# Attention and a gated feed-forward block: a new order of the steps, and GpSimd waiting for VectorE at a port that both use

## The chip, the cores and the metric

The kernel runs on one core of one Trainium2 chip. The metric is the device time of one execution in microseconds (us); it is given as the median of three runs. The engines are TensorE (PE; its weight loads are PEld), VectorE (DVE), ScalarE (ACT), GpSimd (POOL) and SyncE (SP), which issues all DMAs here.

## The reference

Attention over 8 batches of 12 heads, 448 positions and 64 columns, with `q` and `k` normalised by row, then a feed-forward block with a convolution of three taps over the sequence inside its gate:

```python
def rmsnorm(x, g):
    rms = np.sqrt(np.mean(x * x, axis=-1, keepdims=True) + 1e-06)
    return x / rms * g
q_n, k_n = (rmsnorm(q, g_q), rmsnorm(k, g_k))
scores = scale * np.matmul(q_n, k_n.transpose(0, 1, 3, 2))
attn = softmax(scores)
x = np.matmul(attn, v)          # 8 x 448 x 768 after heads are joined
h = np.maximum(x @ w_in, 0.0)   # 768 -> 1024
gate = 1.0 / (1.0 + np.exp(-conv3(h)))
out = h * gate @ w_out          # 1024 -> 768
```

## The kernel before

Two heads form a pair; there are 48 pairs `n`, six of them a batch `b`. A pair is loaded as rows of `q`, `k` and `v`. Its `q` and `k` are squared (`square`), summed (`square_sum`, L396) and turned into a factor by nine small steps (`rsqrt`, L404; L417 to L432 are its instructions), with which `apply_rms` (L440) multiplies them; that product is recorded under the helper's line L110 with the tile `sq`. Transposes on TensorE (L456) and copies (`qk_hi`, `qk_lo`, tiles `kT` and `qT`) follow, from pair 10 on a transposing DMA for `q` in place of one of them. `scores` (L642) go to PSUM, seven blocks of rows `j` a pair; for each of them `soft_max` (L648, VectorE) takes the row maximum and `soft_exp` (L656, ScalarE) the exponential with its row sum. From pair 10 on a value is carried as two float16 halves, a high and a low one: `p_hi` copies to float16 and `p_lo` (L669) subtracts the copy from the value, tile `ph`, again under L110; `p_turn` (L676) then transposes both halves by a DMA to tile `PT`. Blocks that are not transposed so go over TensorE (L686). `v_hi` and `v_lo` (L746, instruction at L748, tile `vp`) do the same with `v`; `pv` (L764) multiplies. `sum_add`, `sum_step` and two small DMAs spread the reciprocal row sums (`rB`), `x_scale` (L775) applies them, `x_hi` and `x_lo` (L786) split the result.

The feed-forward block of a batch starts when its six pairs are done: `in_part` (L848) and `out_part` (L917) are its matmuls, three for each product of halves, and `in_relu`, `in_conv`, `in_tanh`, `in_gate`, `in_hi`, `in_lo` work on each of its eight column blocks. Its matmuls are interleaved with the attention of later batches. Its weights arrive as float64 words and are converted by bit operations on VectorE (`convert`, L269, three instructions a part at L221, L225, L229), then bounded: ScalarE takes the largest magnitude of each part (L279), `bound_max` (L286) the largest of all, `bound_turn` (L289) turns it over TensorE (L190), and a power of two scales the weight, which `split` and `rest` cut in halves. `x @ w_in` can start after that.

All of this is some thousands of steps with a time each, a place in a plan (`at`), shifted by the table `SHIFT`. A planner inside the kernel (the loop at L1473) orders them before anything is emitted: it plays the engines forward with a duration for each step from the table `options`, picks on each engine the waiting step with the least sum of start and urgency, and where a step may run on several engines takes the one that would start first, with a patience from `PH` added for the second choice. `shared` (L1460) tells which steps it takes to need the SBUF port that VectorE and GpSimd have in common; before, one such step on either engine held back the other until it was nearly done, in the plan:

```python
            end = t + c
            free[e] = end - OVER[e]
            if shared(e, step[0]):
                port = free[e] - 0.08
```

In the emitted program an engine runs its instructions in the order so found, and waits for another engine only where the data demand it. The plan's port rule thus set the order, and no instruction waited for it.

Of the kernel before, what the change touches and what calls it, by code (L numbers as in the profile page):

```python
# [20 lines left out]
    sw=0.0, f_pl=0.052, f_ql=0.872, f_lo=0.172, f_rms=0.091, f_sq=0.309, T=17.368, ti=41.151,  # L21
    si=4.096, so=8.649, hop=0.891, beta=0.015, wi0=-53.559, wi1=121.264, wo0=27.379,
    wo1=191.814, cw=130.244, p_evac=0.84, p_hi=0.797, p_lo=1.64, p_rms=0.176, p_v=3.888,
    p_x=0.778, p_g=2.422, p_relu=5.177, p_cv=2.905, p_ev=1.195, sp=0.047, nbulk=4, p_rs=0.042,
    p_sq=15.42, p_w=72.367, v0=26.835, nd=6, cs=5, ct=3, cm=9, ne=5, n2=0, n1=10, q1=10, nf=10,
    pvs=4, p_sa=1.065, p_c0=0.206, p_ca=0.624, p_ss=3.937, p_qh=3.454, p_ql=2.719, p_ph=4.9,
    p_pl=4.316,
)
PACE = [
    19.684, 19.21, 17.229, 18.732, 12.899, 14.504, 12.3, 10.264, 22.811, 17.751, 23.834, 17.246,  # L30
]
SHIFT = dict(
    prepare=49.118, load_g=66.183, make_g=161.271, load_cw=41.777, make_cw=228.436, load=30.589,
    convert=88.08, bound=185.211, bound_max=505.945, bound_turn=109.494, bound_row=36.478,
    bound_spread=103.145, scale=368.594, in_factor=602.484, split=143.452, rest=-5.433,
    out_factor=26.564, load_k=207.53, load_q=-22.481, square=411.214, square_sum=340.919,
    rsqrt=50.152, apply_rms=498.265, qk_transpose=555.031, qk_hi=86.942, v_load=355.244,
    v_bound=-7.228, scores=24.319, soft_max=-4.096, soft_exp=21.811, p_transpose=365.136,
    p_evac=1.005, sum_add=366.28, sum_step=2.99, sum_transpose=104.607, sum_evac=262.686,
    sum_store=184.116, sum_load=7.026, pv=384.832, x_scale=90.761, x_hi=276.516, x_lo=5.432,  # L40
    v_max=-27.973, v_turn=484.625, v_row=103.578, v_spread=219.686, v_scale=143.146,
    qk_lo=-5.353, q_hi=-16.467, q_lo=93.092, q_turn=368.336, p_hi=513.085, p_lo=-4.651,
    p_turn=292.059, p_low=-2.554, v_hi=204.989, v_lo=184.473, moe_scales=122.854,
    in_part=120.167, in_relu=338.096, in_conv=209.998, in_tanh=27.902, in_gate=21.022,
    in_hi=197.514, in_lo=1.938, in_carry=175.792, out_scales=185.546, out_part=267.736,
    out_evac=257.905, out_store=1.003,
)
SCHED = {}
# [21 lines left out]
def tile_attention_moe(ctx: ExitStack, tc, q, k, v, g_q, g_k, w_in, conv_w, w_out, out):  # L70
# [1203 lines left out]
    def options(name, *a):  # L1274
# [21 lines left out]
            square=lambda: [act(1.06), pool(1.89)] if a[1] == 2 else [act(0.55), pool(1.05)],  # L1296
            square_sum=lambda: [dve(1.21 if a[1] == 2 else 0.62)],
            rsqrt=lambda: [dve(0.19)] if a[1] == 1 or n0 and not a[2] else [dve(0.19), pool(0.54 if a[1] in (4, 7, 8) else 0.28)],
            apply_rms=lambda: [dve(0.69), pool(1.07)] if n0 else [pool(1.07), dve(0.69)],
            qk_transpose=lambda: [pe(0.42)],  # L1300
            qk_hi=lambda: [act(0.6), dve(0.62)],
            qk_lo=lambda: [dve(0.65)],
# [287 lines left out]
```

## Time and profile before

| | |
|---|---|
| runs, us | 843.82, 840.89, 843.28 (median 843.28) |
| profiled execution, span, us | 844.4 |
| its own time beside the span | not given by the page; the span is the first to the last instruction |
| mean granted clock of TensorE | 0.994 |
| PE / DVE / ACT / POOL busy, us | 799.5 / 701.8 / 698.1 / 517.7 |

The page gives busy time by engine as a union of its instructions' spans. Matmuls overlap each other in the records, so a TensorE that is busy throughout is not at its peak. A row of the timeline gives start, length, engine, line and output<-input; in brackets the idle time before it and what ended that. The chain is followed back from the last instruction.

### The profile page before, as it was taken

The numbers are of one execution on the slowest core, as the hardware profiler recorded it, in microseconds if no ns is written. First come the engines' busy times: TensorE is split into PE (matmuls) and PEld (weight loads), VectorE is DVE, ScalarE is ACT, GpSimd is POOL, SyncE is SP. The second block draws the span as 40 slices with busy tenths as digits, with TensorE's granted clock in tenths as the row PEclk, the third lists the DMA queues.
The fourth block names the chain that finished last, engine by engine and source line by source line (L and its number), as shares of the span: only waits on it lengthen the run. The fifth ranks groups of instructions, "written<-read, shape, count | busy, mean of one in ns | idle before, by whom it ended". The sixth has DMA issues, their size and how long they took to land.

```text
span 844.4 us, 17078 instructions
## 1 busy us (share of the span) xinstructions
PE 799.5 (95%) x5650; PEld 435.0 (52%) x5650; DVE 701.8 (83%) x1298; ACT 698.1 (83%) x1647; POOL 517.7 (61%) x633
## 2 busy tenths in 40 slices
PE   3897999999999999999999999999999999999998
PEld 2454455545554555555555555555545555555554
DVE  7889988997899889998889988998789989781430
ACT  4889999989899887999898987998898987893441
POOL 4445246487678667597577767697667767572120
PEclk9998999999999999999999999999999999999999
DMA  9684553169997899869997898979996899555001
GB/s 255 180 197 122 172 147 109 45 137 197 180 194 173 163 193 200 167 141 196 197 177 161 182 200 186 179 150 199 183 187 154 185 184 169 108 106 112 10 18 58
DMA packets 325640, 132.47 MB, mean 157 GB/s; under 512 B 265312, under 2 KB 321968, under 8 KB 325552
## 3 DMA queue, kind: packets, MB, share of 16 engines
q1 hardware_dynamic: 325552, 131.39, 75.0%
q8 instruction: 44, 0.72, 0.4%
q14 instruction: 44, 0.36, 0.1%
HBM read 56.65 MB, written 11.18 MB: 80 GB/s over the span
## 4 chain that ended last, share of the span: by engine, by line
PE 38%; ACT 24%; DVE 17%; DMA 9%; issue 7%; POOL 4%; SPq 2%; ACTq 0%; DVEq 0%; POOLq 0%
PE bank L917 15%; PE bank L848 8%; PE bank L764 6%; PE bank L642 5%; DMA rB<-rd 4%; ACT ph L98 3%; PE bank L686 3%; ACT sq L385 2%; DMA PT<-ph 2%; DMA wo<-in_moe_w_in_dram 2%; DVE vp L748 1%; ACT PT L98 1%; POOL ph L110 1%; ACT bank L856 1%; SPq L678 1%
## 5 line engine op out<-in xcount | busy, mean ns | idle before, releaser
L848 PE MATMUL bank<-x,wi 128*128 128x448 f16 x1152 | 233.8, 353 | 0.0
L917 PE MATMUL bank<-wo,gring 128*128 128x384 f16 (+1 forms) x1056 | 203.4, 327 | 1.8 <-DVE c_(0_7_1979 L878 1.7
L848 PEld LDWEIGHTS <-wi 128*128 128x128 f16 x1152 | 110.9, 98 | 99.3 <-issue 7.6
L917 PEld LDWEIGHTS <-gring 128*128 128x128 f16 (+1 forms) x1056 | 101.6, 99 | 67.6 <-issue 16.3
L642 PE MATMUL bank<-kT,qT 64*128 64x448 f16 (+3 forms) x1072 | 131.8, 395 | 4.1 <-ACT qT L98 3.4
L764 PE MATMUL bank<-PT,vp 112*64 112x448 f16 x912 | 93.7, 354 | 0.8 <-DVE c_(5_4_8472 L878 0.4
L110 POOL TENSOR_TENSOR x<-x,x 128x448 f16<-128x448 f32 x48 | 52.9, 1102 | 45.3 <-ACT x L98 33.3
L110 POOL TENSOR_TENSOR sq<-qkf,st 112x512 f32<-112x512 f32 x61 | 72.1, 1191 | 8.5 <-DVE st L417 5.1
L764 PEld LDWEIGHTS <-vp 112*64 112x64 f16 x912 | 50.2, 110 | 41.3 <-issue 12.6
L396 DVE TENSOR_REDUCE st<-sq 112x16 f32<-112x1024 f32 (+1 forms) x50 | 58.2, 1168 | 7.0 <-ACT sq L385 6.5
L642 PEld LDWEIGHTS <-qT 64*128 64x128 f16 (+1 forms) x912 | 32.7, 97 | 51.8 <-issue 32.1
L385 ACT ACTIVATE sq<-qkf 112x1024 f32<-112x1024 f32 (+1 forms) x50 | 51.1, 1022 | 4.2 <-DMA qkf<-in_q_dram 2.3
L917 PE MATMUL bank<-wo,wi 128*128 128x384 f16 (+1 forms) x192 | 46.9, 326 | 0.0
L456 PE MATMUL bank<-ident,sq 112*128 112x112 f32 x232 | 32.4, 267 | 14.4 <-POOL sq L110 13.9
L775 DVE TENSOR_TENSOR x<-bank,rB 128x448 f32<-128x448 f32 x38 | 23.6, 622 | 25.2 <-PE bank L764 9.9
L702 DVE TENSOR_TENSOR PT<-bank,PT 112x512 f16<-112x512 f32 x57 | 39.0, 684 | 4.3 <-ACT PT L98 3.9
L856 ACT ACTIVATE bank<-bank 128x448 f32<-128x448 f32 x64 | 34.1, 534 | 7.3 <-PE bank L848 6.6
L748 DVE SCALAR_TENSOR_TENSOR vp<-v,vsc,vp 112x512 f16<-112x512 f32 x38 | 39.8, 1047 | 0.2 <-ACT vp L102 0.2
L98 ACT COPY PT<-bank 112x512 f32<-112x512 f32 x64 | 36.9, 590 | 3.5 <-PE bank L686 3.4
L110 DVE TENSOR_TENSOR sq<-qkf,st 112x512 f32<-112x512 f32 x35 | 38.7, 1131 | 0.0
L709 POOL TENSOR_SCALAR rsum<-rsum 128x7 f32<-128x7 f32 x48 | 17.5, 365 | 33.5 <-ACT e_(3_6_774 L656 7.5
L98 ACT CAST x<-x 128x448 f16<-128x448 f32 x45 | 25.2, 560 | 15.5 <-DVE x L775 14.8
(2228 smaller groups left out, 2021.8 us busy)
## 6 DMA issues: line engine op xcount, KB each, us to landing
qkf<-in_k_dram SPq DMA_DIRECT2D x48, 224.0 KB
v<-in_v_dram SPq DMA_DIRECT2D x48, 224.0 KB
rB<-rd SPq DMA_DIRECT2D x96, 112.0 KB
wo<-in_moe_w_in_dram SPq DMA_DIRECT2D x12, 512.0 KB
gring<-in_moe_w_out_dram SPq DMA_DIRECT2D x16, 384.0 KB
qkf<-in_q_dram SPq DMA_DIRECT2D x24, 224.0 KB
qkf<-in_q_dram SPq DMA_DIRECT2D x48, 112.0 KB
PT<-ph SPq DMA_TRANSPOSE x209
```

What stands on the lines that cost most here:

```text
L98: (nc.scalar.copy if e == "ACT" else elementwise(e).tensor_copy)(dst, src)
L110: elementwise(e).tensor_tensor(dst, a, b, op=op)
L385: nc.scalar.activation(sq, x, AF.Square)
L396: nc.vector.tensor_reduce(st, sq, axis=AX.X, op=ALU.add)
L456: nc.tensor.transpose(ps[:, t * PB : (t + 1) * PB], x[:, t], ident[:PB, :PB])
L642: nc.tensor.matmul(ps[u][o, :S], lhs, rhs, start=(i == 0), stop=(whole(m) or i == 2),)
L702: nc.vector.tensor_tensor(turned(n, j, 1), held["t", ("p", n, j)][:PB].rearrange("p (k q) -> p k q", k=NB), turned(n, j, 0), op=ALU.subtract,)
L748: nc.vector.scalar_tensor_tensor(vp[:, 1], old("v", n), old("vsc", n // NP)[:PB, 1:2], vp[:, 0], op0=ALU.mult, op1=ALU.subtract,)
L764: nc.tensor.matmul(ps[HALF[h], :S], lhs, rhs, start=(i == 0 and k == 0), stop=(i == pvs(n)[-1] and k == NB - 1),)
L848: nc.tensor.matmul(ps[:, :S], wi[:, wl, c, fc * P : (fc + 1) * P], old("x", b * NP + c)[:, xl], start=(i == 0), stop=(i == 3 * NP - 1),)
L856: nc.scalar.activation(ps, ps, AF.Relu, scale=2.0 ** -24)
L917: nc.tensor.matmul(ps[p0 : p0 + m, :NO2], g, wo[:, wl, fc, half * NO2 : (half + 1) * NO2], start=(i == 0), stop=(i == 3 * NFC - 1),)
```

## The change

The change has three parts.

First, the planner's durations (`options`) are replaced by others (60 or so of them), and `PH`, `PACE` and `SHIFT` by other numbers, so that the order on every engine and the choice of engines come out anew. Of these tables a line or two:

```diff
-    sw=0.0, f_pl=0.052, f_ql=0.872, f_lo=0.172, f_rms=0.091, f_sq=0.309, T=17.368, ti=41.151,
+    sw=0.0, f_pl=0.0372, f_ql=0.301, f_lo=0.0904, f_rms=0.0813, f_sq=0.2875, T=17.3632,
...
-    prepare=49.118, load_g=66.183, make_g=161.271, load_cw=41.777, make_cw=228.436, load=30.589,
+    prepare=752.847, load_g=657.535, make_g=976.01, load_cw=330.398, make_cw=2.091, load=33.068,
...
-            make_cw=lambda: [dve(2.1)],
+            make_cw=lambda: [dve(0.6)],
...
-            q_lo=lambda: [pool(1.15), dve(0.69)],
+            q_lo=lambda: [pool(1.155), dve(0.8)],
...
-            soft_exp=lambda: [act(0.645)],
+            soft_exp=lambda: [act(0.72)],
```

Second, the port rule in the plan: a step of VectorE that uses the port (`SHARED`) holds back GpSimd until 0.16 us after its end, one of GpSimd (`LOCKS`) holds back VectorE until 0.115 us before its end. Third, the first GpSimd step that the plan puts behind such a VectorE step gets a real wait: its first instruction waits for that step's last one.

```diff
-    pmode, port = None, 0.0
+    pmode, port = None, dict(DVE=0.0, POOL=0.0)
+    turn, held_by = None, {}
...
-        "convert", "rest", "q_hi", "q_lo", "rsqrt", "in_carry", "moe_scales",
+        "convert", "rest", "q_hi", "q_lo", "rsqrt", "in_carry", "moe_scales", "out_scales",
...
-        "q_hi", "rest",
+        "q_hi", "rest", "sum_add",
...
-                    t = max(t, port)
+                    t = max(t, port[e])
...
             if shared(e, step[0]):
-                port = free[e] - 0.08
+                if e == "DVE":
+                    port["POOL"], turn = end + 0.16, step
+                else:
+                    port["DVE"] = end - 0.115
+                    if turn:
+                        held_by[step], turn = turn, None
...
+    owners, traced = set(held_by.values()), {}
+
+    def traced_on(e, start):
+
+        kind = nc.vector.engine if e == "DVE" else nc.gpsimd.engine
+        return [i for i in nc.cur_bb.bb.instructions[start:] if i.engine == kind]
+
     with tc.manual_schedule():
         for step in order:
             taken[:] = placed.get(step, ())
+            start = len(nc.cur_bb.bb.instructions)
             steps[step][2](*step[1:])
+            if step in owners:
+                traced[step] = traced_on("DVE", start)[-1]
+            if step in held_by:
+                tc.add_manual_dep(
+                    traced_on("POOL", start)[0], traced[held_by[step]].name,
+                    mybir.DependencyInfo(mybir.DependencyClass.Sync, mybir.DependencyReason.DATA),
+                    reason="shared port",
+                )
```

What is computed stays the same. TensorE's and SyncE's instructions stay in number. Elementwise steps change engine: VectorE issues 1,389 instructions in place of 1,300, ScalarE 1,251 in place of 1,285, GpSimd 574 in place of 638. The largest groups are `apply_rms` (18 more on VectorE, 18 fewer on GpSimd), `x_lo` (13 more on VectorE), the copy of `kT` (12 from ScalarE to VectorE), `in_carry` (11 from ScalarE to VectorE) and the small steps of `rsqrt` (some 22 net more on VectorE, 30 fewer on GpSimd); `q_lo` goes the other way (5 to GpSimd). Of GpSimd's instructions, 177 in place of 94 wait for VectorE, among them 55 `p_lo`, 16 `x_lo` and 16 `sum_add`, which was 0 for each before.

The order at three places; line numbers after the change are greater by 1. The first is the start, pair 0's two `apply_rms` (`sq_0<-qkf_0`). GpSimd before:

```order
L419 TENSOR_SCALAR st_0_109<-st_0_109 112x8
L420 TENSOR_TENSOR st_0_109<-st_0_109 112x8
L110 TENSOR_TENSOR sq_0_110<-qkf_0_105,st_0_109 112x2x4x64
L423 TENSOR_SCALAR st_1_143<-st_1_143 112x8
L110 TENSOR_TENSOR sq_0_110<-qkf_0_105,st_0_109 112x2x4x64
```

VectorE after the change (L431, L433 and L418 are `rsqrt` steps, L397 the sum over squares of pair 1, L222 and L226 the conversion of `w_in`):

```order
L431 TENSOR_TENSOR st_0_109<-st_0_109 112x8
L111 TENSOR_TENSOR sq_0_110<-qkf_0_105,st_0_109 112x2x4x64
L433 TENSOR_TENSOR st_0_109<-st_0_109 112x8
L397 TENSOR_REDUCE st_1_145<-sq_1_146 112x8
L418 SCALAR_TENSOR_TENSOR st_0_109<-st_0_109 112x8
L222 TENSOR_SCALAR wi32_84<-wo32_85 128x512
L418 SCALAR_TENSOR_TENSOR st_0_109<-st_0_109 112x8
L226 SCALAR_TENSOR_TENSOR wi32_84<-wo32_85,wi32_84 128x512
L111 TENSOR_TENSOR sq_0_110<-qkf_0_105,st_0_109 112x2x4x64
```

The two products moved from GpSimd's queue to VectorE's, where a sum and steps of the conversion stand between them.

The second is `bound_max` of `w_in` (`wred_in`) on VectorE; L225 and L229 (L226, L230 after) are steps of its conversion, `sst_(3_` the `soft_max` of pair 3. Before:

```order
L229 SCALAR_TENSOR_TENSOR wi32_84<-wo32_85,wi32_84 128x512
L648 TENSOR_REDUCE sst_(3_4_706<-bank0_66 128x1
L229 SCALAR_TENSOR_TENSOR wi32_84<-wo32_85,wi32_84 128x512
L648 TENSOR_REDUCE sst_(3_5_725<-bank1_67 128x1
L229 SCALAR_TENSOR_TENSOR wi32_84<-wo32_85,wi32_84 128x512 x2
L648 TENSOR_REDUCE sst_(3_6_739<-bank2_68 128x1
L221 TENSOR_SCALAR wo32_85<-gring_86 128x384 x2
L287 TENSOR_REDUCE wred_in_91<-wamax_90 128x1
L225 SCALAR_TENSOR_TENSOR wo32_85<-gring_86,wo32_85 128x384 x2
L229 SCALAR_TENSOR_TENSOR wo32_85<-gring_86,wo32_85 128x384 x2
```

After the change:

```order
L111 TENSOR_TENSOR sq_4_435<-qkf_4_321,st_4_434 112x2x4x64 x2
L222 TENSOR_SCALAR wi32_84<-wo32_85 128x512
L226 SCALAR_TENSOR_TENSOR wi32_84<-wo32_85,wi32_84 128x512 x3
L230 SCALAR_TENSOR_TENSOR wi32_84<-wo32_85,wi32_84 128x512 x4
L649 TENSOR_REDUCE sst_(3_0_672<-bank2_68 128x1
L544 TENSOR_REDUCE vacc_1_600<-v_7_590 112x1
L288 TENSOR_REDUCE wred_in_91<-wamax_90 128x1
L111 TENSOR_TENSOR sq_5_519<-qkf_5_425,st_4_434 112x2x4x64
L194 TENSOR_REDUCE mx_in_690<-bank3_69 1x1
L649 TENSOR_REDUCE sst_(3_1_692<-bank5_71 128x1
```

The conversion's last steps stand in one run, and `bound_max` moved ahead of six of the pair's seven `soft_max`.

The third is GpSimd in the middle of the program, at pair 30's first `p_lo` (`ph<-e_(30_`), with the engines or DMA queues that each instruction waits for. Before:

```order
L110 TENSOR_TENSOR ph2_80<-e_(30_0_6289,ph2_80 128x4x112 [waits DMAHW5_49,Activation_49,Pool_49]
L432 TENSOR_TENSOR st_32_6141<-st_32_6141 112x32 [waits Pool_49]
L110 TENSOR_TENSOR ph3_81<-e_(30_1_6314,ph3_81 128x4x112 [waits DMAHW0_49,Activation_49]
L110 TENSOR_TENSOR sq_32_6142<-qkf_32_5735,st_32_6141 112x2x4x64 [waits DVE_49,PE_49]
L110 TENSOR_TENSOR x_28_6380<-x32_28_6368,x_28_6380 128x448 [waits Activation_49]
L110 TENSOR_TENSOR qkf_32_5735<-sq_32_6142,qkf_32_5735 112x512 [waits Activation_49]
L110 TENSOR_TENSOR ph0_78<-e_(30_2_6342,ph0_78 128x4x112 [waits DMAHW5_49,Activation_49]
```

After the change:

```order
L111 TENSOR_TENSOR ph2_80<-e_(30_0_6281,ph2_80 128x4x112 [waits DMAHW5_49,Activation_49,Pool_49]
L433 TENSOR_TENSOR st_32_6129<-st_32_6129 112x32 [waits DVE_49,Pool_49]
L433 TENSOR_TENSOR st_32_6129<-st_32_6129 112x32 [waits DVE_49]
L111 TENSOR_TENSOR ph3_81<-e_(30_1_6301,ph3_81 128x4x112 [waits DMAHW1_49,DVE_49,Activation_49]
L111 TENSOR_TENSOR x_28_6370<-x32_28_6363,x_28_6370 128x448 [waits DVE_49,Activation_49]
L111 TENSOR_TENSOR sq_33_6226<-qkf_33_6082,st_32_6129 112x2x4x64 [waits DMAHW0_49,DMAHW7_49,DVE_49,PE_49]
L111 TENSOR_TENSOR ph0_78<-e_(30_2_6327,ph0_78 128x4x112 [waits DMAHW5_49,Activation_49]
```

One `p_lo`, `x_lo` of pair 28 and `apply_rms` of pair 33 now wait for VectorE, and a first-half product of pair 32 is gone from this queue.

## Rows read from the trace of the kernel before

**Rows 1.** The page: busy time by engine, and the chain's shares by engine.

```profile
PE 799.5 (95%) x5650; PEld 435.0 (52%) x5650; DVE 701.8 (83%) x1298; ACT 698.1 (83%) x1647; POOL 517.7 (61%) x633
...
PE 38%; ACT 24%; DVE 17%; DMA 9%; issue 7%; POOL 4%; SPq 2%; ACTq 0%; DVEq 0%; POOLq 0%
```

**Rows 2.** Windows: span, then each engine's busy us, TensorE's clock, DMA share, GB/s.

```profile
60.00:80.00 20.00, 15.65 (x80) 10.44 (x80) 19.60 (x38) 18.41 (x44) 10.08 (x15) 0.83 0.53 130
...
100.00:300.00 200.00, 191.81 (x1349) 102.55 (x1350) 180.70 (x348) 182.09 (x443) 135.06 (x171) 1.00 0.71 151
300.00:500.00 200.00, 194.15 (x1454) 105.04 (x1453) 182.83 (x321) 177.09 (x417) 143.74 (x169) 1.00 0.93 181
500.00:700.00 200.00, 196.15 (x1467) 106.72 (x1467) 179.12 (x323) 176.04 (x414) 142.75 (x173) 1.00 0.91 180
```

**Rows 3.** Tiles `vp`, `sq`: min/median/max ns; the page's groups: busy us, mean ns.

```profile
L748 DVE SCALAR_TENSOR_TENSOR vp<-v,vsc,vp x38: 730/744/3010, 191.7 to 757.2; 112x512 f16<-112x512 f32 x38
...
L110 DVE TENSOR_TENSOR sq<-qkf,st x35: 673/926/2524, 187.0 to 707.0; 112x512 f32<-112x512 f32 x35
...
L748 DVE SCALAR_TENSOR_TENSOR vp<-v,vsc,vp 112x512 f16<-112x512 f32 x38 | 39.8, 1047 | 0.2 <-ACT vp L102 0.2
L110 DVE TENSOR_TENSOR sq<-qkf,st 112x512 f32<-112x512 f32 x35 | 38.7, 1131 | 0.0
```

**Rows 4.** Timeline near 456 us (start, us): `v_lo` (vp), GpSimd's first and last subtraction.

```profile
455.12 1.04 POOL L110 TENSOR_TENSOR ph<-e_(28_1_5884,ph 128x448 f16<-128x448 f32 x1
...
455.79 2.91 DVE L748 SCALAR_TENSOR_TENSOR vp<-v,vsc,vp 112x512 f16<-112x512 f32 x1
...
457.11 1.04 POOL L110 TENSOR_TENSOR ph<-e_(28_2_5899,ph 128x448 f16<-128x448 f32 x1
```

**Rows 5.** Chain in order of time: start, us, what.

```profile
327.15 3.67 DVE sq L110 x2
334.00 2.93 DVE vp L748
...
395.57 2.61 DVE sq L110 x2
...
645.18 2.82 DVE vp L748
```

**Rows 6.** Timeline of the first `apply_rms` on GpSimd and TensorE's wait.

```profile
9.20 1.07 POOL L110 TENSOR_TENSOR sq<-qkf,st 112x512 f32<-112x512 f32 x1 [0.94 <-ACT sq L385]
...
10.32 1.01 PE L456 MATMUL bank<-ident,sq 112*128 112x112 f32 x4 [10.32 <-POOL sq L110]
...
12.24 1.41 POOL L110 TENSOR_TENSOR sq<-qkf,st 112x512 f32<-112x512 f32 x1 [0.88 <-ACT kT L102]
```

**Rows 7.** Timeline before `bound_max` of `w_in`: GpSimd's `apply_rms`, conversions on VectorE.

```profile
58.51 5.12 POOL L110 TENSOR_TENSOR sq<-qkf,st 112x512 f32<-112x512 f32 x4
...
63.18 2.00 DVE L229 SCALAR_TENSOR_TENSOR wi<-wo,wi 128x512 int32<-128x512 int32 x1
...
65.63 1.28 DVE L229 SCALAR_TENSOR_TENSOR wi<-wo,wi 128x512 int32<-128x512 int32 x2
```

**Rows 8.** Waits: us, times, longest; the last from tile `vp`: us, times.

```profile
PE bank L190 <- DVE wred_in L287: 3.5, 1, 3.5
...
SPq L678 <- POOL ph L110: 50.9, 53, 3.2
...
  DMA PT<-ph: 1.5, 4
```

**Rows 9.** Prices of moved steps: VectorE's `rsqrt` and `kT`, GpSimd's `apply_rms`, `x_lo`.

```profile
L417 DVE SCALAR_TENSOR_TENSOR st<-st x44: 147/185/1059, 8.7 to 700.0; 112x32 f32<-112x32 f32 x35, 112x8 f32<-112x8 f32 x9
...
L104 DVE TENSOR_SCALAR kT<-bank,G 128x448 f16<-128x448 f32 x11 | 7.4, 673 | 0.0
...
L110 POOL TENSOR_TENSOR x<-x,x 128x448 f16<-128x448 f32 x48 | 52.9, 1102 | 45.3 <-ACT x L98 33.3
L110 POOL TENSOR_TENSOR sq<-qkf,st 112x512 f32<-112x512 f32 x61 | 72.1, 1191 | 8.5 <-DVE st L417 5.1
```

More of the change, by code (lines that the diff above doesn't have):

```diff
@@ L34 @@
[L34 to L45, printed above, removed]
@@ L46 @@
-    out_evac=257.905, out_store=1.003,
+    prepare=752.847, load_g=657.535, make_g=976.01, load_cw=330.398, make_cw=2.091, load=33.068,
+    convert=493.531, bound=434.297, bound_max=997.493, bound_turn=110.974, bound_row=439.308,
+    bound_spread=144.878, scale=264.777, in_factor=855.239, split=253.006, rest=-5.488,
+    out_factor=6.856, load_k=514.422, load_q=-22.79, square=152.084, square_sum=53.339,
+    rsqrt=129.836, apply_rms=371.449, qk_transpose=946.516, qk_hi=163.782, v_load=526.719,
@@ new lines @@
+    v_bound=-7.992, scores=165.021, soft_max=-3.98, soft_exp=71.301, p_transpose=1089.978,
+    p_evac=1.021, sum_add=292.102, sum_step=3.621, sum_transpose=7.451, sum_evac=951.667,
+    sum_store=442.223, sum_load=7.241, pv=277.343, x_scale=531.668, x_hi=50.036, x_lo=5.449,
+    v_max=-28.59, v_turn=474.043, v_row=421.545, v_spread=561.379, v_scale=1063.291, qk_lo=-6.16,
+    q_hi=-16.404, q_lo=231.56, q_turn=97.487, p_hi=281.925, p_lo=-4.849, p_turn=602.22,
+    p_low=0.089, v_hi=46.398, v_lo=369.031, moe_scales=639.368, in_part=826.195, in_relu=654.815,
@@ L47 @@
+    in_conv=84.909, in_tanh=377.101, in_gate=187.899, in_hi=137.708, in_lo=1.949,
+    in_carry=294.262, out_scales=266.089, out_part=548.912, out_evac=315.656, out_store=-0.364,
 )
@@ L1294, in options @@
             load_k=lambda: [dma("lk", 0.84)],
             load_q=lambda: [dma("lq", 0.45, 2) if n % 2 else dma("lq", 0.9)],
[L1296 to L1299, printed above, removed]
+            square=lambda: [act(1.06), pool(1.89)] if a[1] == 2 else [act(0.63), pool(1.05)],
@@ L1300, in options @@
+            square_sum=lambda: [dve(1.21 if a[1] == 2 else 0.68)],
+            rsqrt=lambda: [dve(0.175)] if a[1] == 1 or n0 and not a[2] else [dve(0.175), pool(0.73 if a[1] in (4, 7, 8) else 0.34)],
+            apply_rms=lambda: [dve(0.68), pool(1.045)] if n0 else [pool(1.045), dve(0.68)],
             qk_transpose=lambda: [pe(0.42)],
-            qk_hi=lambda: [act(0.6), dve(0.62)],
-            qk_lo=lambda: [dve(0.65)],
+            qk_hi=lambda: [act(0.6), dve(0.675)],
+            qk_lo=lambda: [dve(0.675)],
@@ L1555, in tile_attention_moe @@
                 enqueue(s_)
-    SCHED.update(after=after, t=max(done.values()), t0=0.0, done=done, engine=engine, order=order)
+    SCHED.update(held_by=held_by, after=after, t=max(done.values()), t0=0.0, done=done, engine=engine, order=order)
+    owners, traced = set(held_by.values()), {}
+    def traced_on(e, start):
+        kind = nc.vector.engine if e == "DVE" else nc.gpsimd.engine
+        return [i for i in nc.cur_bb.bb.instructions[start:] if i.engine == kind]
     with tc.manual_schedule():
```

68 lines of the change are left out of this document (35 added, 33 removed).

## The prediction

> **What bounds the kernel now.** I read the page's head and its chain first, then TensorE's busy time by stretch, then the chain piece by piece, then single places. The sum below is made against the profiled execution's span of 844.4 us; the page gives no other time for it, and the median of the three runs, 843.28, lies 1.1 us under it, so I take 1.1 off at the end. About 0.5%, here 4.2 us, is what a measurement of this kernel can tell from no change.
>
> TensorE is busy for 799.5 us of the span, yet the chain that ended last runs on TensorE for only 38%: 24% is ScalarE, 17% VectorE, 9% DMA [rows 1]. So TensorE is nearly full, and the gaps that are left are made by the small engines. The reader should see where they are. From 60 to 80 us TensorE is busy for 15.65 of 20 us, with a granted clock of 0.83. From 100 to 700 us it is busy for 191.81 + 194.15 + 196.15 = 582.1 of 600 us, so 17.9 us are idle [rows 2]. The matmuls stay the same, so what can be won lies in the first 80 us and in the 17.9.
>
> VectorE is what this change is about. Its `v_lo` takes 0.744 us in the median, but up to 3.01, and 1.047 in the mean of 38. Its `apply_rms` takes 0.673 at best, 1.131 in the mean of 35 [rows 3]. The excess is 38 x 0.303 = 11.5 us and 35 x 0.458 = 16.0 us. One place shows how it arises: `v_lo` starts at 455.79 and lasts 2.91 us, while GpSimd runs three 1.04 us subtractions end to end, from 455.12 to 458.15; VectorE's instruction ends 0.55 us after the last of them [rows 4]. Such stretched instructions stand on the chain: 3.67 us for two `apply_rms` that need 1.35, 2.61 for another two, and three `v_lo`, of 2.93 and 2.82 us the first and the last [rows 5]. Over their ordinary lengths that is 2.3 + 1.3 + 3 x 2.1 = 9.9 us of the chain, all between 327 and 648 us.
>
> **The change, part by part.** TensorE's order hardly moves and its matmuls stay; SyncE's DMAs stay in number. What changes is which engine has a step, the order on the small engines, and the new waits.
>
> *Start.* The first two `apply_rms` ran on GpSimd for 1.07 and 1.41 us and ended at 10.27 and 13.65; TensorE's first transposes waited for the first of them until 10.32, its second group for the other [rows 6]. They go to VectorE, where one takes at least 0.673 [rows 3]. On paper that is 0.4 + 0.7 us. VectorE's own queue gets them, though, with a sum over squares of the next pair and two steps of weight conversion put between the two, so the first gain is partly spent in the queue. TensorE's first scores follow the second `apply_rms`. Bounds: 1.1 us less, or nothing where the queue eats it. I take -0.5, half-way, as the first place of the order shows the queue both shorter on GpSimd and longer on VectorE.
>
> *First weight.* TensorE loses 3.5 us in the wait for `bound_max` of `w_in` [rows 8]. VectorE is late with it: a step of the conversion, of which two take 1.28 us a little later, takes 2.00 from 63.18, where four GpSimd `apply_rms` have run end to end for 5.12 us [rows 7]. The wait cost 3.5 us, and the clock of 0.83 over 20 us cost up to another 0.17 x 20 = 3.4 [rows 2]. In the new order the rest of the conversion is run in one piece ahead of pair 3's seven `soft_max`, and `bound_max` comes before six of these instead of after all of them. That brings the weight forward and holds pair 3 back: seven conversion steps of 0.64 us [rows 7] are 4.5 us in which no `soft_max` starts. Bounds: 6.9 less, if idle time and low clock both go, and 4.5 more, if the run in one piece is a gap for TensorE. I take -1, near the middle: what is moved ahead and what is put behind are of the same size, and VectorE gets more to do here in any case.
>
> *Work that changes engine.* VectorE gets 18 more `apply_rms` (0.673), 12 copies of `kT` (0.673) and 13 `x_lo`, which I price by those copies, over the same 448 columns [rows 3, 9]: 12.1 + 8.1 + 8.7 = 28.9 us. A net 46 others, mostly `rsqrt` steps (0.185 in the median, [rows 9]), add about 0.2 us each, 9 us. Together some 38 us on VectorE. GpSimd loses 18 x 1.19 and 13 x 1.10 and some 30 small ones, by about 0.25 us each, some 43 us of 517.7 [rows 1, 9]; ScalarE loses 34 instructions, those copies among them. From 100 to 700 us VectorE is busy for 180.70 + 182.83 + 179.12 = 542.7 of 600 us [rows 2]: 57 us are free, and the added work is hidden there only as long as the stretched time goes down as well. If that cover were gone it would cost what the second rival costs.
>
> *The waits, from 100 us on.* About 83 more GpSimd instructions now wait for VectorE, 55 of them `p_lo`, which waited for none before. What stands behind a held `p_lo` is GpSimd's own queue, and on SyncE the transposing DMA `p_turn`, whose queue waited for GpSimd's `p_lo` for 50.9 us already [rows 8]; behind that stand loads and the row sums. TensorE hardly feels it so far: its weight loads for `pv` waited for a transposing DMA four times, 1.5 us in all [rows 8]. For the gain, the bound above is the 9.9 us of stretch on the chain. The bound below is the second rival's loss of 6.5 us. I take half of the upper bound, -5: the port goes to GpSimd in fewer places, but where a stretched step goes, something is late next. In the same stretches ScalarE is busy for 182.09, 177.09 and 176.04 of 200 us each [rows 2], so the next late piece is often a `soft_exp` or a copy of ScalarE that comes a microsecond later.
>
> The Trainium skill (SBUF — State Buffer, "SBUF: two separate sides") says that whichever of a two-input VectorE instruction and a GpSimd instruction starts first holds the shared ports for the whole of it, and the other waits until it ends. By that the three long `v_lo` could be stretched by one GpSimd instruction each, 1.04 us and not 2.1, the upper bound would be 3.6 + 3 x 1.04 = 6.7 and my term -3.4. The `v_lo` of [rows 4] was kept out by two GpSimd instructions that started after it, so the measurement decides, and I keep -5.
>
> *Sum:* 844.4 - 0.5 - 1 - 5 = 837.9 of span, less 1.1: **836.8 us**, 0.8% under the runs.
>
> **The rivals.** *The waiting changes sides.* The two engines still want the ports for the same instructions, and what VectorE no longer waits, GpSimd does; the moved steps only trade 1.1 us on one engine for 0.67 on the other. For it: GpSimd's `p_lo` is followed by a DMA and then `pv`, which is also a path to TensorE. Against it: GpSimd is busy for 61% and VectorE for 83%, and GpSimd's mark on the chain is 4% to VectorE's 17% [rows 1]. Then only the first two terms stay: 844.4 - 1.5 - 1.1 = 841.8, no change. The Trainium skill (SBUF — State Buffer, "Who interferes with whom") has this as a rule: the order of issue decides who blocks, so an order can move the wait but not remove it. By that rule alone this rival would be the forecast; [rows 4], where one VectorE instruction paid for three of GpSimd, speaks against it.
>
> *VectorE becomes the bound.* The new waits hit instructions that were not the cause, the stretched ones stay, and VectorE carries 38 us more. It decides as soon as the stretch that goes is less than the work that comes; the two groups above hold only 27.5 us of stretch, so this is near. VectorE has 17% of the chain [rows 1]; at that share 38 us cost 6.5, and 844.4 - 1.5 + 6.5 - 1.1 = 848.3, slower. Against it: 57 us are free on VectorE from 100 to 700 us.
>
> *Transposes come late.* A held `p_lo` costs up to one VectorE step of 0.67 us, and 55 of them over the 38 pairs that need them are 1.4 per pair, or 1.0 us. If 0.3 of that reached each `pv`, 38 x 0.3 = 11 us would be added: 844.4 - 1.5 + 11 - 1.1 = 853. It decides when TensorE's waits for that DMA, now 1.5 us, pass the gain of 5.
>
> **How the numbers follow.** Forecast 0.58, the waiting changes sides 0.24, VectorE the bound 0.12, late transposes 0.06. The forecast with its bounds reaches from 828 (a full 10 us from the waits and 4 from the first weight: 844.4 - 0.5 - 4 - 10 - 1.1 = 828.8, rounded down) to 841; the first rival to 845; the second puts the upper end at 847. So 828 to 847, with about 0.06 left out below and 0.13 above. Faster by over 0.5%, under 839.1, is most of the forecast, 0.50, and 0.02 of the first rival; slower, over 847.5, is 0.09 of the second rival, the third's 0.06 and 0.02 of the first; 0.31 lies between.
>
> **What would show it.** In the changed profile the mean of `v_lo` on VectorE should fall from 1.047 to under 0.85 and that of `apply_rms` from 1.131 to under 0.95; VectorE's busy time should be 700 to 730 us, GpSimd's about 470; TensorE's idle time from 100 to 700 us about 13 us, not 17.9; its wait before the first transposes should end by 10.3 us, and the wait for `bound_max` of `w_in` should not be longer than 3.5 us. The forecast is wrong if these means stay where they are, if VectorE passes 740 us, or if TensorE is seen to wait for the transposing DMA for over 5 us.

## The result, and the profile after

The changed kernel takes 830.07 us in the median (828.91 to 832.17, 4 runs), the kernel before, beside it, 843.55. The ratio is 0.985, with an interval of 0.9827 to 0.9874. So it is 13.5 us faster. The forecast was 6.5 us faster, 836.8: the sign and the range were right, and the gain came out about twice as large. The profiled span is 829.1 us against 844.4, 15.3 less, and the rows below add up to that. Some 2 of these 15.3 us are scatter: in every run that lists both, the span is 1.7 to 2.2 us under the run's time (829.1 belongs to 830.94), so the profiled execution of before took about 846 us, an estimate, 2.7 above the median. The 1.1 that the forecast took off stands for this scatter and not for something outside the span.

The head of the page of the changed kernel, and the chain's shares by engine, answer to [rows 1]:

```profile
PE 795.0 (96%) x5650; PEld 434.0 (52%) x5650; DVE 688.6 (83%) x1387; ACT 687.6 (83%) x1613; POOL 451.1 (54%) x569
...
PE 59%; DVE 13%; ACT 13%; DMA 7%; issue 5%; POOL 2%; SPq 1%; ACTq 0%; POOLq 0%; DVEq 0%
```

VectorE issues 89 instructions more and is busy for 13.2 us less. GpSimd is busy for 66.6 us less. The chain runs on TensorE for 59% of the span and not for 38%: ScalarE's share fell from 24% to 13%, VectorE's from 17% to 13%.

The windows of the changed kernel (span, busy us of PE, PEld, DVE, ACT and POOL, then clock, DMA share, GB/s) answer to [rows 2]:

```profile
60.00:80.00 20.00, 16.52 (x74) 9.22 (x74) 19.55 (x45) 17.91 (x41) 3.89 (x9) 0.83 0.49 122
...
100.00:300.00 200.00, 195.92 (x1388) 106.53 (x1386) 185.62 (x380) 185.40 (x449) 114.55 (x146) 1.00 0.75 155
300.00:500.00 200.00, 197.61 (x1494) 108.20 (x1492) 176.32 (x343) 176.24 (x413) 136.05 (x167) 1.00 0.92 184
500.00:700.00 200.00, 198.39 (x1497) 108.08 (x1495) 177.95 (x343) 174.99 (x410) 139.31 (x171) 1.00 0.91 183
```

TensorE's idle time from 100 to 700 us fell from 17.9 us to 600 - 591.9 = 8.1, so 9.8 of the 15.3 are there. In the first 100 us it was busy for 77.45 us in place of 76.45, 1.0 less idle, at the same low clock of 0.83 from 60 to 80. The idle time behind 700 us did not change. The other 4.5 us are busy time, 799.5 against 795.0 for the same matmuls: the page's largest groups, `in_part` and `out_part`, overlap more closely at the same mean length (233.8 to 231.3 us and, for the part that reads `gring`, 203.4 to 200.0). Up to 1.7 us of it can be the clock, whose mean was 0.996 here and 0.994 before (0.002 x 844.4, an estimate). The two lines of before, then the two of after:

```profile
L848 PE MATMUL bank<-x,wi 128*128 128x448 f16 x1152 | 233.8, 353 | 0.0
L917 PE MATMUL bank<-wo,gring 128*128 128x384 f16 (+1 forms) x1056 | 203.4, 327 | 1.8 <-DVE c_(0_7_1979 L878 1.7
...
L849 PE MATMUL bank<-x,wi 128*128 128x448 f16 x1152 | 231.3, 353 | 0.1
L918 PE MATMUL bank<-wo,gring 128*128 128x384 f16 (+1 forms) x1056 | 200.0, 327 | 0.0
```

Lengths on VectorE answer to [rows 3]; first tile rows (min/median/max in ns), then the groups of lines (busy us, mean ns):

```profile
L111 DVE TENSOR_TENSOR sq<-qkf,st x53: 669/684/1527, 9.7 to 694.0; 112x512 f32<-112x512 f32 x53
L749 DVE SCALAR_TENSOR_TENSOR vp<-v,vsc,vp x38: 729/744/1230, 189.9 to 740.3; 112x512 f16<-112x512 f32 x38
...
L111 DVE TENSOR_TENSOR sq<-qkf,st 112x512 f32<-112x512 f32 x53 | 39.0, 762 | 0.1
L749 DVE SCALAR_TENSOR_TENSOR vp<-v,vsc,vp 112x512 f16<-112x512 f32 x38 | 29.5, 776 | 0.4 <-ACT vp L103 0.4
```

`v_lo` fell from 1.047 us in the mean to 0.776, its longest from 3.01 to 1.23. `apply_rms` fell from 1.131 to 0.762: 53 of them now cost what 35 did. GpSimd's instructions did not grow in turn, but for one group: its `apply_rms` (line 111, 43 of them) takes 1.065 us and not 1.191, its `x_lo` 1.160 and not 1.102 (35 of them for 48).

The first 70 us did not go as they were priced. On VectorE and TensorE (timeline rows: start, us, engine; the short row of L643, the first scores, is of the chain):

```profile
9.68 0.68 DVE L111 TENSOR_TENSOR sq<-qkf,st 112x512 f32<-112x512 f32 x1
...
12.09 0.68 DVE L111 TENSOR_TENSOR sq<-qkf,st 112x512 f32<-112x512 f32 x1
...
10.51 0.98 PE L457 MATMUL bank<-ident,sq 112*128 112x112 f32 x4 [10.51 <-DVE st L433]
12.91 0.98 PE L457 MATMUL bank<-ident,sq 112*128 112x112 f32 x4 [1.43 <-DVE sq L111]
14.52 3.40 PE bank L643 x8
...
61.35 0.27 PE L191 MATMUL bank<-ident,wred_in 128*1 128x128 f32 x1 [1.23 <-DVE wred_in L288]
...
68.94 1.78 PE L643 MATMUL bank<-kT,qT 64*128 64x448 f32 x2 [1.46 <-DVE wo L230]
...
70.83 1.06 PE L687 MATMUL bank<-ident,e_(3_2_730 128*112 128x128 f32 x4
```

and of the kernel before, TensorE's timeline, the chain's row of the first scores, and the row of tile `wred_in`:

```profile
13.71 1.01 PE L456 MATMUL bank<-ident,sq 112*128 112x112 f32 x4 [2.38 <-POOL sq L110]
15.34 1.91 PE bank L642 x4
...
62.30 0.65 PE L686 MATMUL bank<-ident,e_(3_2_661 128*112 128x128 f32 x4
...
L287 DVE TENSOR_REDUCE wred_in<-wamax x1: 165/165/165, 67.9 to 67.9; 128x1 f32<-128x12 f32 x1
```

The first `apply_rms` is 0.39 us shorter, as forecast, but starts 0.48 us later in its new queue and ends at 10.36 us instead of 10.27 [rows 6]. The second comes sooner: its transposes start at 12.91 and not at 13.71, 2.40 us after the first group's and not 3.39, and the first scores at 14.52 and not at 15.34. `bound_max` of `w_in` comes at 61.13 us instead of 67.9, and TensorE waits 1.23 us for it and not 3.5 [rows 8]. But at 68.94 it stands idle for 1.46 us. The trace puts this down to a step of the next weight's conversion, and the wait of the same matmul's weight load to a `soft_exp` of pair 3; which of the two held it is not shown. Pair 3 is late there in any case: its third block is transposed at 70.83 us and not at 62.30, so what was brought forward is paid for elsewhere.

The transposes stayed out of it. SyncE's queue waited for `ph` a little less than before [rows 8], and TensorE's weight loads for `pv` waited for the DMA once, for 0.4 us (the first row is of the waits, the second of tile `vp`):

```profile
SPq L679 <- POOL ph L111: 44.8, 45, 2.7
...
  DMA PT<-ph: 0.4, 1
```

It was ScalarE that waited longer for these DMAs: its `p_hi` copies (tile `ph`) stood for 19.8 us behind them, in 23 places, against 11.2 us in 12 before.

### The profile page after: what moved, and what is told of

The parts are those of the page before. It is cut to its first block, busy times and chain, and to the rows that moved or that the text cites. A ratio compares the mean times of both kernels' runs of the same rounds, so it can differ in the third digit from the quotient of the medians.

```text
span 829.1 us, 17139 instructions
## 1 busy us (share of the span) xinstructions
PE 795.0 (96%) x5650; PEld 434.0 (52%) x5650; DVE 688.6 (83%) x1387; ACT 687.6 (83%) x1613; POOL 451.1 (54%) x569
## 4 chain that ended last, share of the span: by engine, by line
PE 59%; DVE 13%; ACT 13%; DMA 7%; issue 5%; POOL 2%; SPq 1%; ACTq 0%; POOLq 0%; DVEq 0%
PE bank L918 25%; PE bank L849 11%; PE bank L643 8%; PE bank L765 8%; PE bank L687 5%; DMA PT<-ph 3%; ACT ph L99 2%; PE bank L457 2%; DMA rB<-rd 2%; POOL ph L111 1%; DVE st L397 1%; DMA qkf<-in_q_dram 1%; DVE PT L703 1%; ACT sq L386 1%; ACT bank L857 1%
## 5 line engine op out<-in xcount | busy, mean ns | idle before, releaser
L849 PE MATMUL bank<-x,wi 128*128 128x448 f16 x1152 | 231.3, 353 | 0.1
L918 PE MATMUL bank<-wo,gring 128*128 128x384 f16 (+1 forms) x1056 | 200.0, 327 | 0.0
L643 PE MATMUL bank<-kT,qT 64*128 64x448 f16 (+3 forms) x1072 | 131.7, 391 | 3.2 <-DVE wo L230 1.5
L765 PEld LDWEIGHTS <-vp 112*64 112x64 f16 x912 | 48.5, 110 | 42.5 <-issue 11.2
L397 DVE TENSOR_REDUCE st<-sq 112x16 f32<-112x1024 f32 (+1 forms) x50 | 58.2, 1166 | 5.9 <-ACT sq L386 5.9
L111 POOL TENSOR_TENSOR x<-x,x 128x448 f16<-128x448 f32 x35 | 40.6, 1160 | 37.2 <-ACT x L99 20.4
L643 PEld LDWEIGHTS <-qT 64*128 64x128 f16 (+1 forms) x912 | 32.7, 97 | 48.8 <-issue 29.4
L111 POOL TENSOR_TENSOR sq<-qkf,st 112x512 f32<-112x512 f32 x43 | 45.4, 1065 | 16.5 <-issue 6.8
L457 PE MATMUL bank<-ident,sq 112*128 112x112 f32 x232 | 32.9, 268 | 16.5 <-DVE st L433 10.5
L111 POOL TENSOR_TENSOR qkf<-sq,qkf 112x512 f16<-112x512 f32 x34 | 40.7, 1201 | 6.6 <-DMA PT<-ph 2.4
L710 POOL TENSOR_SCALAR rsum<-rsum 128x7 f32<-128x7 f32 x43 | 13.5, 315 | 50.4 <-ACT qT L99 10.1
L457 PEld LDWEIGHTS bank<-ident,sq 112*128 112x128 f32 x232 | 25.5, 143 | 26.6 <-issue 15.5
```

What stands on the lines that cost most here:

```text
L111: elementwise(e).tensor_tensor(dst, a, b, op=op)
L397: nc.vector.tensor_reduce(st, sq, axis=AX.X, op=ALU.add)
L457: nc.tensor.transpose(ps[:, t * PB : (t + 1) * PB], x[:, t], ident[:PB, :PB])
L643: nc.tensor.matmul(ps[u][o, :S], lhs, rhs, start=(i == 0), stop=(whole(m) or i == 2),)
L765: nc.tensor.matmul(ps[HALF[h], :S], lhs, rhs, start=(i == 0 and k == 0), stop=(i == pvs(n)[-1] and k == NB - 1),)
L849: nc.tensor.matmul(ps[:, :S], wi[:, wl, c, fc * P : (fc + 1) * P], old("x", b * NP + c)[:, xl], start=(i == 0), stop=(i == 3 * NP - 1),)
```

## The experiments

My theory after the result: the added waits keep GpSimd's instructions out of VectorE's way, which takes the stretch out of VectorE's instructions, and what comes after 100 us is theirs. The rival: the new order and choice of engines do it, with or without waits. A ratio below is always to the kernel before on the same chip (843.1 to 843.6 us in the median each time), with its 95% interval.

**The waits taken away.** Same order on every engine, no dependencies:

```diff
-            if step in held_by:
+            if False:
                 tc.add_manual_dep(
```

> The changed kernel, its order unchanged on every engine, without the added dependencies of GpSimd on VectorE. Theory (the waits keep the two engines apart, and the gain after 100 us is theirs): the mean of v_lo goes back from 0.775 us to 0.95 or more and that of apply_rms on VectorE from 0.762 to 1.0 or more, and the time is 836 to 842 us. Rival (the new order, with its other choice of engines, already keeps them apart): v_lo stays under 0.85 and apply_rms under 0.85, and the time is 829 to 832 us.

Measured: 839.9 us, 0.9962 (0.9948 to 0.9976). Lengths on VectorE, as above:

```profile
L111 DVE TENSOR_TENSOR sq<-qkf,st 112x512 f32<-112x512 f32 x53 | 50.0, 969 | 0.1
L749 DVE SCALAR_TENSOR_TENSOR vp<-v,vsc,vp 112x512 f16<-112x512 f32 x38 | 33.5, 883 | 0.7 <-ACT vp L103 0.7
```

The time lies in the theory's band. The means lie between the two expectations: `v_lo` lost two fifths of its fall, `apply_rms` a little over half. So in this order the waits are worth 9.8 us of the 13.5 (9.4 by the two ratios, give or take 2.3), and the order without them 3.2 (0.38%, under what I count as a difference, though the interval leaves out 1). Since both kernels issue the same instructions in the same order, they can be matched one by one: without the waits 45 of VectorE's are longer by more than 0.15 us, 32.8 us in all, and 14 are shorter, by 7.4. On GpSimd 43 are longer, by 19.5 us, and 8 shorter, by 5.6. The waits cost neither engine in length.

The traces divide the gain otherwise than the times. The page's head and the window from 100 to 700 us, without the waits:

```profile
PE 798.1 (95%) x5650; PEld 435.6 (52%) x5650; DVE 711.2 (85%) x1387; ACT 689.1 (82%) x1613; POOL 466.7 (56%) x569
...
100.00:700.00 600.00, 589.35 (x4334) 321.50 (x4331) 553.73 (x1060) 534.01 (x1263) 396.19 (x478) 1.00 0.85 173
```

TensorE is idle there for 10.7 us, against 17.9 before and 8.1 with the waits, and the span is 835.8 us. By spans the order gives 8.6 us and the waits 6.7 (1.0 of it idle time in the first 100 us, where TensorE starts 0.85 us later, 2.6 idle time from 100 to 700, 3.1 busy time). But each trace is one execution: this span is 2.3 us under the median of its kernel's spans (838.1), that of the changed kernel 0.9 over (828.2), that of before about 2.7 over, by the estimate above. With these taken out the parts are some 3.6 and 9.9 us again. So the sizes are taken from the medians, and how much of the fall in idle time is the order's, these traces can't tell.

One place shows how the waits work; without them:

```profile
325.97 2.53 DVE L749 SCALAR_TENSOR_TENSOR vp<-v,vsc,vp 112x512 f16<-112x512 f32 x1
...
325.92 1.04 POOL L111 TENSOR_TENSOR ph<-e_(20_1_4037,ph 128x448 f16<-128x448 f32 x1
326.92 1.04 POOL L111 TENSOR_TENSOR x<-x,x 128x448 f16<-128x448 f32 x1
```

and the same instructions in the changed kernel:

```profile
322.05 0.74 DVE L749 SCALAR_TENSOR_TENSOR vp<-v,vsc,vp 112x512 f16<-112x512 f32 x1
...
322.90 1.87 DVE L111 TENSOR_TENSOR sq<-qkf,st 112x512 f32<-112x512 f32 x3
...
320.89 1.04 POOL L111 TENSOR_TENSOR ph<-e_(20_1_4037,ph 128x448 f16<-128x448 f32 x1 [0.24 <-ACT ph L99]
322.93 2.75 POOL L111 TENSOR_TENSOR x<-x,x 128x448 f16<-128x448 f32 x1 [1.01 <-DVE vp L749]
```

Without the wait `v_lo` is kept out by two GpSimd instructions and ends 0.54 us after the second. With it, `x_lo` stands until `v_lo` is through, and `v_lo` takes 0.74. Then `x_lo` pays 1.7 us behind three `apply_rms`; but GpSimd is busy for 54% of the span and VectorE for 83%.

**The waits alone, in the old order.**

```diff
                 port = free[e] - 0.08
+                if e == "DVE":
+                    turn = step
+                elif turn:
+                    held_by[step], turn = turn, None
...
+            if step in held_by:
+                tc.add_manual_dep(
```

> The kernel before, its order unchanged on every engine, with the added dependencies alone, set by the same rule from its own plan. Theory of the waits: the mean of v_lo falls from 1.047 us to under 0.85, that of apply_rms from 1.131 to under 0.9, and the time is 834 to 840 us. Rival (the order): the means fall, but GpSimd's held steps are late where the order did not plan for it, and the time is 842 to 848 us.

Measured: 846.14 us, 1.0034 (1.0015 to 1.0053), the rival's band. The windows from 100 to 700 us are, for this kernel,

```profile
100.00:700.00 600.00, 581.06 (x4246) 313.44 (x4247) 532.60 (x983) 534.15 (x1266) 406.95 (x509) 1.00 0.86 170
```

VectorE is busy there for 10 us less than before, GpSimd for 14.6 less, and TensorE is idle for 18.9 us, not less than the 17.9 of before. Matched one by one with the kernel before, 41 VectorE instructions are shorter, by 33.8 us, and 40 others longer, by 22.4. A held GpSimd step comes later and meets the next VectorE instruction instead. In its timeline:

```profile
517.95 3.23 DVE L110 TENSOR_TENSOR sq<-qkf,st 112x512 f32<-112x512 f32 x2
...
518.04 1.61 POOL L110 TENSOR_TENSOR qkf<-sq,qkf 112x512 f16<-112x512 f32 x1
519.61 1.03 POOL L110 TENSOR_TENSOR ph<-e_(32_2_6790,ph 128x448 f16<-128x448 f32 x1
```

and in that of the kernel before:

```profile
516.93 1.48 DVE L110 TENSOR_TENSOR sq<-qkf,st 112x512 f32<-112x512 f32 x2
```

These two `apply_rms` took 1.48 us there and take 3.23 here. So the rival of the prediction in which the waiting changes its place does happen, in the order that was not made for the waits. The Trainium skill (SBUF — State Buffer, "Who interferes with whom") has the order of issue decide who blocks; that agrees with this run. That an order could only move the wait was the prediction's own inference, and the run without waits speaks against it: there an order together with waits removed part of it.

**The rule and the numbers, each alone.** Two kernels plan anew: one with the new durations and numbers but the old single port, no dependencies (first piece); one with the old durations and numbers under the new rule, with dependencies (second piece, the first line of its tables). Both are shown against the changed kernel.

```diff
-                if e == "DVE":
-                    port["POOL"], turn = end + 0.16, step
-                else:
-                    port["DVE"] = end - 0.115
-                    if turn:
-                        held_by[step], turn = turn, None
+                port = free[e] - 0.08
...
-    sw=0.0, f_pl=0.0372, f_ql=0.301, f_lo=0.0904, f_rms=0.0813, f_sq=0.2875, T=17.3632,
+    sw=0.0, f_pl=0.052, f_ql=0.872, f_lo=0.172, f_rms=0.091, f_sq=0.309, T=17.368, ti=41.151,
```

> The new durations and tables of numbers with the old single port rule in the plan and without dependencies; this gives an order of its own. Theory of the waits: long v_lo and apply_rms as before (means over 0.95), time 838 to 848 us. Rival (the gain is in the measured durations and the new numbers, whatever the port rule): 829 to 834 us.

> The old durations and tables of numbers with the new port rule in the plan and with the dependencies; this gives an order of its own. Theory of the waits: means of v_lo and apply_rms under 0.85, time 834 to 842 us, although the numbers were not chosen for this order. Rival (the numbers carry the gain): 843 to 852 us, with means that are just as short.

Measured: 862.05 us, 1.0231 (1.0198 to 1.0264), outside both bands and slower than anything else, with the long means that the theory named (1.098 for `v_lo`, 1.296 for `apply_rms`); and 839.13 us, 0.9949 (0.9929 to 0.9969), as the theory had it, with means of 0.821 (`v_lo`) and 0.795 (`apply_rms`). Under the old rule and without waits the new numbers are no gain.

The second of them without its dependencies, and the first with them (the edits are those of the first two experiments):

> The old durations and numbers with the new port rule in the plan, without the dependencies: the order of the run that gave 839.13 us, its waits taken away. Theory (waits pay in an order that plans for them): 845 to 852 us, since here too the waits should be worth 6 to 12 us. Rival (what the plan's rule keeps apart stays apart by itself): 837 to 841 us.

> The new durations and numbers with the old single port rule in the plan (862.05 us without dependencies), now with the dependencies set from that plan. If the dependencies pay only in a plan that leaves room for the handover, as the order of before shows (846.14 against 843.11): 860 to 866 us. If they pay wherever long stretches stand (v_lo has a mean of 1.098 us there): 848 to 856 us.

Measured: 853.79 us, 1.0121 (1.0074 to 1.0169), a little beyond the theory's band, and 848.74 us, 1.0083 (1.0066 to 1.0101), the second case of its expectation. All eight cases together, medians in us, some from different chips, on each of which the kernel before took 843.1 to 843.6 (the lists `SHARED` and `LOCKS` are the old ones in the first line alone):

| numbers, rule of the plan | without waits | with waits | the waits' part |
|---|---|---|---|
| old, old (the kernel before) | 843.1 | 846.1 | +3 |
| old, new | 853.8 | 839.1 | -14.7 |
| new, old | 862.1 | 848.7 | -13.3 |
| new, new (the change) | 839.9 | 830.1 | -9.8 |

In three of four orders the waits are worth 10 to 15 us, and my idea that they need the new rule in the plan fell with the third line: they pay there too, where the plan leaves 0.32 us less for the handover (0.16 before the end of VectorE's step, in place of 0.16 behind it). Only the order of before does not gain by them; its loss of 3 us, 0.34%, is again under what I count as a difference, though the interval leaves out 1. Why that one is the exception, no run here settles.

**Which waits.** The changed kernel with the dependency on `p_lo` alone, and on all held steps but `p_lo`:

```diff
-            if step in held_by:
+            if step in held_by and step[0] == "p_lo":
```

> The changed kernel, its order unchanged, with the added dependencies kept on p_lo alone. By the runs without any and with all of them, these dependencies are worth some 10 us here. Theory (p_lo is the GpSimd step that keeps VectorE out, as in the stretched v_lo of the trace before): 830 to 834 us, v_lo mean under 0.82. Rival (the other held steps, apply_rms, x_lo, in_lo, sum_add, matter as much): 834 to 838 us.

> The changed kernel, its order unchanged, with the added dependencies on every held step but p_lo. Theory (p_lo is what matters): 836 to 840 us, near the 839.9 without any. Rival (the other held steps matter as much): 832 to 836 us.

Measured: 836.03 us, 0.9916 (0.9891 to 0.9942), and 837.74 us, 0.9923 (0.9898 to 0.9949). The two do not agree on the theory. The first missed its band, and its mean of `v_lo`, 0.838 us, missed the 0.82; the second lies in the theory's band and not in the rival's. The two gains over the kernel without waits, 3.9 and 2.2 us, can't be told apart by their intervals. Neither half gives the 9.8 us alone, and whether `p_lo` matters more than the others stays open. That the two give more together than their sum (6.0 against 9.8) lies within the intervals.

**Waits in both directions.** The first shared VectorE step behind a locking GpSimd step waits for it too:

```diff
                 if e == "DVE":
                     port["POOL"], turn = end + 0.16, step
+                    if back:
+                        gate_by[step], back = back, None
                 else:
-                    port["DVE"] = end - 0.115
+                    port["DVE"], back = end - 0.115, step
...
```

> The changed kernel with a dependency in the other direction too: the first shared VectorE step behind a GpSimd step that locks the port waits for it, so that the two engines never ask for the port at once where the plan kept them apart. If VectorE's instructions are still stretched by GpSimd (means of 0.776 and 0.762 us against 0.729 and 0.669 at best), this takes the rest of the stretch: 826 to 829 us. Rival (a wait for the end of a GpSimd step costs VectorE as much as the stretch, and the instructions behind it wait too): 831 to 838 us.

Measured: 835.28 us, 0.9899 (0.9848 to 0.995). The lengths and waits of VectorE, and the windows from 100 to 700 us:

```profile
L111 DVE TENSOR_TENSOR sq<-qkf,st 112x512 f32<-112x512 f32 x53 | 35.0, 687 | 12.6 <-POOL x L111 4.5 <-POOL qkf L111 3.6 <-POOL ph L111 1.9
L749 DVE SCALAR_TENSOR_TENSOR vp<-v,vsc,vp 112x512 f16<-112x512 f32 x38 | 28.4, 746 | 5.1 <-POOL ph L111 4.3 <-POOL qkf L111 0.5
...
100.00:700.00 600.00, 589.06 (x4341) 320.77 (x4340) 523.38 (x1060) 534.31 (x1264) 376.21 (x478) 1.00 0.86 173
```

The time is 5.2 us above the changed kernel's, in the rival's band, with intervals that overlap by a little. The stretch is nearly gone, VectorE is busy there for 16.5 us less than in the changed kernel, and TensorE is idle for 10.9 us instead of 8.1. What these two groups save in length, 4.0 + 1.1 us, they lose in waits, 12.6 + 5.1. So a short instruction is not the aim by itself; what VectorE, the fuller engine, waits before it starts counts as well.

**How much is the order itself?** Three more plans: the handover planned at 0.08 us in place of 0.16, the new durations with the old numbers, and one weight nudged.

```diff
-                    port["POOL"], turn = end + 0.16, step
+                    port["POOL"], turn = end + 0.08, step
...
-    ti=41.2236, si=4.107, so=8.3066, hop=0.89068, beta=0.014927, wi0=-54.4573, wi1=123.1391,
+    ti=41.2236, si=4.107, so=8.3066, hop=0.89068, beta=0.014930, wi0=-54.4573, wi1=123.1391,
```

> The changed kernel with one number of the plan's rule nearer to the trace: GpSimd's step is planned 0.08 us behind the end of VectorE's, the pause that held steps of the trace show, and not 0.16; the dependencies stay. This gives an order of its own. If the time of the plan is what counts, and a better number makes a better plan: 826 to 831 us. Rival (any new order of these thousands of steps loses what was found by choosing numbers for one order): 833 to 845 us.

> The new measured durations, with the new port rule and the dependencies, but with the old PH, PACE and SHIFT. Beside the run with old durations too (839.13 us) it shows the durations alone. Theory (durations nearer to the trace make a better plan): 832 to 837 us. Rival (the numbers were chosen for one set of durations, and another set only shuffles the order): 839 to 850 us.

> The changed kernel with one weight of the planner's choice, beta, 0.014930 in place of 0.014927; all else, the dependencies too, as it is. Nothing of the mechanism changes, only the order, from some point on. It shows how far two orders that are equal in kind lie apart: within 2 us (828 to 832), and then the differences of the other orders of several us are causes; or 834 to 842, and then a good part of what the new numbers gave is the choice of one order out of many.

Measured: 839.75 us, 0.9963 (0.9945 to 0.9981); 849.39 us, 1.0083 (1.0062 to 1.0105); and 830.82 us, 0.9861 (0.9844 to 0.9879). The nudged kernel equals the changed one; VectorE's order differs only from some 470 us on, so it speaks for the later part of the program alone. In the other two the order is new throughout, the waits are in, and the lengths are nearly as short as in the changed kernel. For the one with 0.08:

```profile
L111 DVE TENSOR_TENSOR sq<-qkf,st 112x512 f32<-112x512 f32 x53 | 40.1, 784 | 0.1
L749 DVE SCALAR_TENSOR_TENSOR vp<-v,vsc,vp 112x512 f16<-112x512 f32 x38 | 30.4, 799 | 0.5 <-ACT vp L103 0.4
```

Yet it loses 9.7 us to the changed kernel, and the other 19.3. So my theory is half the cause: given an order (but for that of before), the waits are worth 10 to 15 us, and the stretch goes with them; between orders, differences just as large do not come from the stretch of these groups, and durations nearer to the trace are no gain as long as the numbers were chosen for other ones. Which of the numbers carry it was not tried.

## Why the prediction was right, and where it was not

- **Waits from 100 us on, -5 (bounds -9.9 and +6.5).** The mechanism was right and the term mis-sized. What came after 100 us is 14.3 us of the span (9.8 of TensorE's idle time, the rest taken to be its denser work) or, by the medians, 13.5 less 1.0 in the first 100 us, 12.5. The waits are worth 9.8 us over the whole run, a figure that is the same as that idle time by chance, and the order the rest. So the bound, "2.3 + 1.3 + 3 x 2.1 = 9.9 us of the chain", held for the waits. The step that failed is the half taken of it, and besides that the new order had no term of its own after 100 us: work that changes engine was called hidden, and TensorE's order was said hardly to move. The reason for the half, that something else is late next, was not borne out: ScalarE, which was named, has 13% of the chain and not 24%. That 9.9 and 9.8 are so near is partly luck: the bound counted the longest pieces of one chain of the kernel before, and the run without waits shows the effect spread over 45 instructions of VectorE and 32.8 us.
- **Start, -0.5.** About right in size. The first transposes start at 10.51 us and not at 10.32, the miss that the text named as a sign, but one trace can't tell so little: in the six traced runs whose queues begin as the changed kernel's do (it, the run with one weight nudged, and those that take away or add waits) they start between 10.33 and 11.77. What is steady is the second group: it starts 2.40 to 2.41 us after the first in all six, against 3.39 before and 3.00 in the old order with waits. So 0.6 to 1.0 us came from the second `apply_rms`, and what the queue did to the first is open.
- **First weight, -1.** `bound_max` did come sooner, by 6.8 us, and 2.3 us of its wait went. The low clock of 0.83 stayed, another wait of 1.5 us stands 7.6 us later, and with the start the first 100 us give 1.0 us of idle time in all, not 1.5.
- **Work that changes engine, hidden.** Right, and with more room than I counted: VectorE was to be busy for 700 to 730 us and is for 688.6. I held against its 38 us of new work 27.5 us of stretch in two groups; its busy time fell by 13.2 in spite of that work, so some 51 us went, an estimate, much of it in small steps: the `rsqrt` product (line 418) takes 0.232 us in the mean (over 112x32) and took 0.383. `x_lo` costs 0.616 there, not 0.673. GpSimd was to be near 470 and is at 451.1.
- **The signs.** The means of `v_lo` (0.776, under 0.85) and `apply_rms` (0.762, under 0.95) and the wait for `bound_max` came as written; TensorE's idle time is 8.1 and not about 13.
- **The rivals.** *The waiting changes sides* is false for this change (both engines' instructions got shorter, but for GpSimd's `x_lo`) and true for the old order with waits. *VectorE becomes the bound* is out with 688.6 us, *late transposes* with 0.4 us of waits for the DMA. The Trainium skill (SBUF — State Buffer, "SBUF: two separate sides") lets whichever starts first hold the ports for its whole instruction, the other waiting until it ends. That would have made the term -3.4, further off than -5, and the `v_lo` of 2.53 us above, kept out by a second GpSimd instruction, differs from it again.

## What to carry to other kernels

Where two engines want one port, let the emptier one wait for the fuller one, by a real dependency; adding the other direction gave back some 5 of their 10 us here. Judge it in the order in which it will run: waits by the same rule were worth 10 to 15 us in three orders of this kernel and nothing, or a loss of 3, in a fourth, and a whole new order moves the time by as much at nearly the same lengths. So a new order needs a term of its own in the sum. And one profiled execution is one draw: lay its span beside the times of the other runs before its rows are split into parts.

## What was not expected of the hardware

The port can be kept, in both directions, by what follows back to back. In the run without waits `v_lo` started 0.05 us after GpSimd's `ph`, yet it also sat out the next GpSimd instruction and ended 0.54 us after that one. In the changed kernel `x_lo`, 0.03 us later than the first of three `apply_rms` of VectorE, took 2.75 us against 1.04 ordinarily, and ended 0.91 us after the last of the three. But it is no rule that the whole row goes first. In the trace of before, 35 of VectorE's `v_lo`, `apply_rms` and `q_lo` (tile `qkf`) take over 0.25 us more than 0.744, 0.675 and 0.68 us, their ordinary lengths here and in the changed kernel. Of these, 26 waited only for the one GpSimd instruction that was running, and 9 also sat out one or two that started after them, as in [rows 4]. And 20 of the 35 ended their wait although the next GpSimd instruction stood within 0.05 us behind; there that next one became the longer, as here:

```profile
518.07 1.23 POOL L110 TENSOR_TENSOR ph<-e_(32_2_6790,ph 128x448 f16<-128x448 f32 x1 [0.81 <-ACT ph L98]
518.34 1.52 DVE L748 SCALAR_TENSOR_TENSOR vp<-v,vsc,vp 112x512 f16<-112x512 f32 x1
519.27 1.49 POOL L110 TENSOR_TENSOR sq<-qkf,st 112x512 f32<-112x512 f32 x1
```

What decides whether `v_lo` gets in, no run here shows. All 35 end 0.54 to 0.55 us after the last GpSimd instruction that they sat out. A held instruction that starts 0.14 us behind the end of the one it waited for can still lose the port to the next, as that `x_lo` did.
